# The first tiles of layer 0 in another order: statistics, transposed copies and PSUM banks

## The chip, the cores and the metric

The kernel runs on one core of a Trainium2 chip. Its engines work side by side, each on its own list of instructions in the order of the program: PE (TensorE, matrix products and transposes), DVE (VectorE), ACT (ScalarE), POOL (GpSimd), and SP, which here only issues DMAs. PE writes to PSUM, and a tile in PSUM can be overwritten only when DVE or ACT has read it. The metric is the device time of one execution in microseconds (us). It was 1230.78 us as the median of three runs, from 1225.78 to 1231.24.

## What is computed

Four layers, forward and backward, on x of 2048 rows by 512 columns: a linear attention block A, a gated block B, then A and B again with the same weights. Each adds to the residual stream. Outputs are the result and the gradients of x and of the five weight matrices.

```python
def _A_ref(x, wqkv, wo):                       # H = 32 heads, Dh = 16
    q, k, v = split(x @ wqkv)
    phi = lambda t: jnp.where(t > 0, t + 1, jnp.exp(t)) + 1e-6
    pq, pk = phi(q), phi(k)
    kv = jnp.einsum("bhsd,bhse->bhde", pk, v)
    z = jnp.einsum("bhsd->bhd", pk)
    o = einsum(pq, kv) / (einsum(pq, z)[..., None] + 1e-6)
    return o @ wo
def _B_ref(x, w_gate, w_up, w_down):
    return (_sigmoid(x @ w_gate) * (x @ w_up)) @ w_down
x = x + _A_ref(_layernorm(x), A_wqkv, A_wo)
x = x + _B_ref(_layernorm(x), B_w_gate, B_w_up, B_w_down)
...
_out, _vjp = jax.vjp(_f, A_x, A_wqkv, A_wo, B_w_gate, B_w_up, B_w_down)
return (_out, *_vjp(grad_out))
```

## The kernel before

The rows are cut into 16 tiles of 128. The change lies in `kq_fwd`, in the part that runs for layer 0 alone; this is the first thing that the kernel does. For each tile `st` it makes k and q from the normalised x, applies phi, and gathers X, the sum over all tiles of h-transposed times phi(k), from which the block's later matrices come.

One tile passes through these steps:

- `ln.stats(st)` (L436 to L442, in `ln_stats`): DVE takes the mean and variance in two instructions (L436, L438), then POOL makes of them, in three instructions, the reciprocal deviation (L439 and the power on L440) and the shift (L442).
- `ln.apply(st)` (L447): one ACT instruction writes the normalised tile into `h_all`.
- `stage_hT(sts, evac)`: PE transposes four blocks of 128 columns for each tile in `sts` into the PSUM tile `hT_tp` (L522), and one copy brings them to SBUF as `hTst`; it is made by DVE (L350, `evac` "vector") or by ACT (L352, "scalar"). `hT_tp` has one buffer, so that the next transposes wait for the copy. After the tile that ends a group of four a DMA stores the group (L585).
- `proj(st, 1)` and `proj(st, 0)`: four matmuls each (L591) for k and for q. They go into PSUM tiles handed out by `mm_tile` in the fixed turn t, t, y (two buffers of pool t, one of y).
- `exp_to` (L608): ACT takes the exponential of k, and another of q. `clamp` (L611): one DVE instruction for both halves of `a_t`, which has three buffers and is free again when its store to DRAM has landed. `phi_out` (L614): one DVE instruction for k and one for q; they also set the PSUM tiles free. `save_phq` (L617) stores the q half, and after tiles 2, 5, 8 and 11 the loads of later weights are issued behind that store.
- `X_some`: three or four X matmuls (L599) for tiles two back, into four PSUM tiles `X_ps` of the pools g and u.

No planner chooses the order: the engines' lists follow the order of calls in the loop. In iteration `st` the loop calls proj for k, the exponential of k, a staging of transposes (one tile at a time up to tile 3, then two at a time in odd iterations, copied by ACT), proj for q, the exponential of q, `ln.apply(st + 3)`, clamp and both phi, and then `ln.stats(st + 5)`. Before the loop stand the statistics of tiles 0 to 3 and the applies of 0 to 2; iteration 0 also runs `ln.stats(4)`. After the loop a sum of phi(k) over all rows (L708, 16 matmuls) goes into the next tile of the same turn of banks.

Of the kernel before, what the change touches and what calls it, by code (L numbers as in the profile page):

```python
# [10 lines left out]
F32 = mybir.dt.float32  # L11
# [7 lines left out]
D = 512  # L19
# [3 lines left out]
P = 128  # L23
NST = S // P
NDC = D // P
# [37 lines left out]
def ps_tile(k, which, shape, dt, name):  # L63
    return k.ps[which].tile(shape, dt, name=name, tag="ln_tp" if which == "ln" else f"{which}_ps")
# [3 lines left out]
def kernel(  # L68
# [78 lines left out]
    with tc.tile_pool(name="wfwd", bufs=1, reuse_waits="tile") as wfwd, ExitStack() as lctx, tc.manual_schedule(engines=EM):  # L147
# [44 lines left out]
        with tc.tile_pool(name="aq0", bufs=1, reuse_waits="tile") as aq:  # L192
            A = kq_fwd(k, aq, 0, lns[0], lns[1], x_bf)
            with tc.tile_pool(name="wt_stage", bufs=2, reuse_waits="tile") as wt_stage:
                fill = Fill(wT_groups_a(k, wt_stage))
                A.tail(fill)
                ab_fwd(k, A, lns[1], fill, nxt=lns[2])
        xctx.close()
        with tc.tile_pool(name="aq2", bufs=1, reuse_waits="tile") as aq:
            A = kq_fwd(k, aq, 2, lns[2], lns[3])  # L200
            hctx.close()
            wb = bctx.enter_context(tc.tile_pool(name="wbwd", bufs=1, side="right", reuse_waits="tile"))
# [340 lines left out]
def kq_fwd(k, aq, l, ln, ln_next, x_src=None):  # L543
# [10 lines left out]
    with ExitStack() as ctx:  # L554
# [13 lines left out]
        def mm_tile():  # L568
            nm = "tty"[cnt[0] % 3]
            cnt[0] += 1  # L570
            return ps_tile(k, nm, [P, D], F32, f"{nm}_mm")

        def stage_hT(sts, evac):
            st0 = sts[0]
            if st0 >= NST:
                return
            if st0 % NB == 0 or (st0 == 2 and ln.early):
                hTs["cur"] = stg.tile([P, NB, NDC, P], BF16, name="hTst")
            lo, n = st0 % NB, len(sts)
            for st in sts:  # L580
                hTs[st] = hTs["cur"][:, st % NB, :, :]
            ln.transposes(hTs["cur"][:, lo:lo + n, :, :].rearrange("p n c t -> p (n c) t"), sts, evac)
            if sts[-1] % NB == NB - 1:
                b, a = sts[-1] // NB, 2 if ln.early and sts[-1] < NB else 0
                nc.sync.dma_start(out=sv["hT"][(b * NB + a) * P:(b + 1) * NB * P, :].rearrange("(n p) d -> p n d", p=P),  # L585
                                  in_=hTs["cur"][:, a:NB, :, :].rearrange("p n c t -> p n (c t)"))

        def proj(st, n, ps=None):
            ps = ps or mm_tile()
            for kc in range(NDC):  # L590
                nc.tensor.matmul(ps[:], lhsT=hTs[st][:, kc, :], rhs=k.wqkv[:, kc, n * D:(n + 1) * D],  # L591
                                 start=(kc == 0), stop=(kc == NDC - 1))
            return ps

        X_ps = []
# [6 lines left out]
        def X_some(n, upto):  # L602
            while n > 0 and Xq and Xq[0][0] <= upto:
                X_mm(*Xq.pop(0))
                n -= 1

        def exp_to(e, ps):
            nc.scalar.activation(e, ps[:], ACT.Exp)  # L608

        def clamp(a, e):  # L610
            nc.vector.tensor_scalar(a, e, 1.0, EPS, ALU.min, ALU.add)  # L611

        def phi_out(out, ps, a):
            nc.vector.scalar_tensor_tensor(out, ps[:], 1.0 + EPS, a, ALU.add, ALU.max)  # L614

        def save_phq(st, a):
            ins = nc.sync.dma_start(out=sv["phq"][rows(st), :], in_=a)  # L617
            if l == 0 and st in k.late_loads:
                with tc.issue_after(ins.ins):
                    k.late_loads[st]()  # L620

        def store_pk(st):
            if st % NB == NB - 1:
                b = st // NB
                nc.sync.dma_start(out=dram_batch(sv["pk"], b), in_=pk_all[:, b * NB:(b + 1) * NB, :])

        def qa_tiles():
            if l == 0:
                return (work.tile([P, 2, D], BF16, name="e_t", bufs=2)[:, 1, :],
                        work.tile([P, 2, D], BF16, name="a_t", bufs=3)[:, 1, :])  # L630
            return (work.tile([P, D], BF16, name="e_t", bufs=4)[:],
                    work.tile([P, D], BF16, name="aq_t", bufs=4)[:])
# [12 lines left out]
        if l == 0:  # L645
            warm_ps = ps_tile(k, "g", [P, P], F32, "warm_ps")
            for i in range(WARM):
                nc.tensor.matmul(warm_ps[:], lhsT=k.ident[:], rhs=k.ident[:], start=True, stop=True)
            nc.scalar.activation(k.tab[:], k.neg[:], ACT.Exp)
            ln.stats(0)  # L650
            k.load_x()
            ln.stats(1)
            ln.apply(0)
            stage_hT([0], "vector")
            for st in range(2, 4):
                ln.stats(st)
            for st in range(1, 3):
                ln.apply(st)
        else:
            hTs.update(ln.early)  # L660
        X_ps += [ps_tile(k, "gu"[i % 2], [P, D], F32, "X_ps") for i in range(NDC)]
        for st in range(NST):
            both = st < NST - QLATE
            ps_k = proj(st, 1)
            if l == 0:
                e_t = work.tile([P, 2, D], BF16, name="e_t", bufs=2)
                a_t = work.tile([P, 2, D], BF16, name="a_t", bufs=3)
                ek, ak, eq, aqt = e_t[:, 0, :], a_t[:, 0, :], e_t[:, 1, :], a_t[:, 1, :]
            else:
                ek = work.tile([P, D], BF16, name="e_t", bufs=4)[:]  # L670
                ak = work.tile([P, D], BF16, name="ak_t", bufs=1)[:]
            exp_to(ek, ps_k)
            if l == 0 and st < 3:
                stage_hT([st + 1], "vector")
            elif l == 2 and st == 0:
                stage_hT([2, 3], "vector")
            elif st % 2 == 1 and st >= 3:
                stage_hT([st + 1, st + 2], "vector" if l == 2 and st % 4 == 1 else "scalar")
            if l == 2 or not both:
                clamp(ak, ek)  # L680
                phi_out(pk_all[:, st, :], ps_k, ak)
            if both:
                ps_q = proj(st, 0)
                if l == 2:
                    eq, aqt = qa_tiles()
                exp_to(eq, ps_q)
            if l == 0:
                ln.apply(st + 3)
                if both:
                    clamp(a_t[:], e_t[:])  # L690
                    phi_out(pk_all[:, st, :], ps_k, ak)
            elif st in (1, 2):
                ln.apply(NST - 3 + st)
            if both:
                if l == 2:
                    clamp(aqt, eq)
                phi_out(A.pq_all[:, st, :], ps_q, aqt)
                save_phq(st, aqt)
            if l == 0:
                if st == 0:  # L700
                    ln.stats(4)
                ln.stats(st + 5)
            store_pk(st)
            X_some(XSTEP + (st % 2 if l == 0 else 0), st - 2)

# [1002 lines left out]
```

## Time and profile before

| what | value |
|---|---|
| profiled execution's own time | 1234.76 us |
| its span | 1233.0 us |
| median of three runs | 1230.78 us |
| PE busy over the span | 1185.6 us, 96% |
| DVE, ACT, POOL busy | 731.7, 597.7, 258.4 us |
| first q,k matmul of layer 0 | at 7.19 us |
| sum of phi(k) begins (L708) | at 55.36 us |

The profile is one execution. The timeline lists instructions in order of start: start and duration in us, engine, line, operation, what is written and read. In brackets stands the idle time of the engine just before, and what ended it. PEld is the weight load of TensorE, SPq the issue of a DMA. The view by stretches gives for each engine its busy us and number of instructions, then the clock that TensorE was granted (1.00 is full), the share of the DMA engines and GB/s.

### The profile page before, as it was taken

To read this page: it belongs to the slowest core of one execution; us is meant where nothing else is said; L and a number is where in the kernel's file an instruction comes from. 1 tells how busy PE (TensorE), PEld (TensorE's weight loads), DVE (VectorE), ACT (ScalarE), POOL (GpSimd) and SP (SyncE) were. 2 spreads that over 40 slices of the span, in tenths; PEclk is the share of its full clock that TensorE was granted. 3 is DMA by queue.
4 is the path that set the end of the run, shared out by engine and by line. 5 is a ranking of instruction groups with operands and counts; after the bars stand their busy time and mean duration, and the time that the engine had idled before them with its cause. 6 is when DMAs were issued, how large, how long until landed. Compare 5 with 4: busy or idle time off the path is not lost.

```text
span 1233.0 us, 21735 instructions
## 1 busy us (share of the span) xinstructions
PE 1185.6 (96%) x8209; PEld 721.2 (58%) x8326; DVE 731.7 (59%) x1411; ACT 597.7 (48%) x1105; POOL 258.4 (21%) x469
## 2 busy tenths in 40 slices
PE   7989999998999999899999999999999999989998
PEld 4445555455555555455555578855557655537877
DVE  6688886777777456564966630156665947621111
ACT  5677777557676645344626631254445536610000
POOL 4246765105665300000100010000000101100000
PEclk9999999999999999999999999999999999998989
DMA  7934454435545867968665768568958765578773
GB/s 248 291 127 157 164 198 171 159 120 182 201 138 203 285 204 228 331 203 274 201 193 155 229 215 280 113 181 277 323 171 279 226 222 177 154 214 260 232 211 108
DMA packets 266233, 256.05 MB, mean 208 GB/s; under 512 B 43280, under 2 KB 251024, under 8 KB 261264
## 3 DMA queue, kind: packets, MB, share of 16 engines
q1 hardware_dynamic: 266128, 254.65, 64.6%
q8 instruction: 65, 1.06, 0.4%
q14 instruction: 40, 0.33, 0.1%
HBM read 135.69 MB, written 118.92 MB: 206 GB/s over the span
## 4 chain that ended last, share of the span: by engine, by line
PE 84%; DVE 8%; DMA 2%; issue 2%; SPq 2%; ACT 2%; POOL 1%; POOLq 0%; DVEq 0%; ACTq 0%
PE p_ps L1367 16%; PE dh_ps L1133 12%; PE g_ps L873 6%; PE u_ps L873 6%; PE y_ps L899 6%; PE dhh_ps L1017 6%; PE p_ps L1353 5%; PE dh_ps L1576 4%; PE T_ps L1092 3%; PE GT_ps L1494 2%; PE dp_ps L1469 2%; PE y_ps L818 2%; PE t_mm L591 2%; PE X_ps L599 2%; PE t_tp L887 1%
## 5 line engine op out<-in xcount | busy, mean ns | idle before, releaser
L1367 PE MATMUL p_ps<-p_set,p_a 128*128 128x256 bf16 (+1 forms) x2048 | 214.1, 266 | 3.5 <-DVE dw_stg L1343 3.5
L1367 PEld LDWEIGHTS <-p_a 128*128 128x128 bf16 x2048 | 186.9, 98 | 26.1 <-issue 3.6
L1025 DVE TENSOR_TENSOR dd<-dhh_ps,ssd 128x512 bf16<-128x512 f32 x144 | 82.5, 629 | 141.0 <-PE dhh_ps L1017 130.7
L1096 ACT COPY ddT<-T_ps 128x1024 bf16<-128x1024 bf16 (+1 forms) x96 | 83.0, 867 | 129.6 <-PE T_ps L1092 129.2
L879 POOL TENSOR_TENSOR ssd_t<-hh_t,oms 128x512 bf16<-128x512 bf16 (+1 forms) x96 | 101.6, 1064 | 53.3 <-ACT out_t L219 40.9
L1133 PEld LDWEIGHTS <-ddT 128*128 128x128 bf16 (+1 forms) x704 | 68.0, 98 | 70.0 <-issue 1.1
L991 POOL TENSOR_SCALAR ab<-c 128x2 f32<-128x2 f32 x64 | 12.3, 192 | 460.9 <-DVE junk L988 447.6
L873 PEld LDWEIGHTS <-hT 128*128 128x128 bf16 x768 | 71.2, 98 | 57.9 <-DVE hT L350 1.5
L1343 DVE TENSOR_TENSOR dw_stg<-p_ps,dw_stg 128x512 bf16<-128x512 f32 (+3 forms) x44 | 28.3, 648 | 125.1 <-PE p_ps L1367 85.6
L873 PE MATMUL g_ps<-wg,hT 128*128 128x512 bf16 (+1 forms) x378 | 88.9, 357 | 1.5 <-DVE hT L350 1.2
L873 PE MATMUL u_ps<-wu,hT 128*128 128x512 bf16 x383 | 89.8, 357 | 0.1
L878 DVE TENSOR_TENSOR hh_t<-u_ps,ssd_t 128x512 bf16<-128x512 f32 (+1 forms) x96 | 61.1, 636 | 46.9 <-PE u_ps L873 26.6
L1133 PE MATMUL dh_ps<-wgT,ddT 128*128 128x512 bf16 (+1 forms) x352 | 87.5, 383 | 0.0
L1353 PE MATMUL p_ps<-p_a,p_set 128*128 128x512 bf16 (+1 forms) x343 | 82.6, 388 | 1.4 <-DMA p_set<-sv_hdl 0.9
L983 ACT ACTIVATE t_sb<-dh_ps,rstd_all 128x512 f32<-128x512 f32 x64 | 44.0, 688 | 78.5 <-PE dh_ps L1576 52.4
L1133 PE MATMUL dh_ps<-wuT,ddT 128*128 128x512 bf16 (+1 forms) x351 | 81.2, 379 | 0.1
L899 PE MATMUL y_ps<-wd,hhT 128*128 128x512 bf16 (+1 forms) x327 | 76.2, 379 | 1.9 <-DVE x L901 0.6
L1017 PE MATMUL dhh_ps<-wdT,gT 128*128 128x512 bf16 (+1 forms) x341 | 75.8, 355 | 2.1 <-DVE dd L1025 0.5
L988 DVE SCALAR_TENSOR_TENSOR junk<-t_sb,h_ld 128x512 bf16<-128x512 f32 x64 | 44.0, 688 | 44.6 <-ACT t_sb L983 44.3
L875 ACT ACTIVATE ssd_t<-g_ps 128x512 bf16<-128x512 f32 (+1 forms) x96 | 53.2, 554 | 31.7 <-PE g_ps L873 31.5
L1345 ACT CAST dw_stg<-p_ps 128x512 bf16<-128x512 f32 (+2 forms) x43 | 24.1, 561 | 68.2 <-PE p_ps L1367 61.4
L1353 PEld LDWEIGHTS <-p_set 128*128 128x128 bf16 (+1 forms) x352 | 34.5, 103 | 38.0 <-issue 2.7
(230 smaller groups left out, 2132.8 us busy)
## 6 DMA issues: line engine op xcount, KB each, us to landing
p_set<-sv_hdd SPq DMA_DIRECT2D x30, 1024.0 KB, 6.3
sv_ssd<-ssd_t SPq DMA_DIRECT2D x32, 688.0 KB, 3.5
ssd<-sv_ssd SPq DMA_DIRECT2D x24, 688.0 KB, 5.1
sv_hdd<-dd SPq DMA_DIRECT2D x48, 320.0 KB, 4.1
sv_hdd<-hh_t SPq DMA_DIRECT2D x32, 320.0 KB, 2.6
h_ld<-sv_h SPq DMA_DIRECT2D x32, 256.0 KB, 4.6
p_a<-sv_h SPq DMA_DIRECT2D x16, 512.0 KB, 6.5
p_set<-sv_dqk SPq DMA_DIRECT2D x8, 1024.0 KB, 7.3
```

The costliest lines, as they stand in the source:

```text
L873: nc.tensor.matmul(ps[:, 0:w], lhsT=hT[:, kc, :], rhs=w_sb[:, kc, c0:c0 + w], start=(kc == 0), stop=(kc == NDC - 1))
L875: nc.scalar.activation(ssd_t[:, 0, c0:c0 + w], g_ps[:, 0:w], ACT.Sigmoid)
L878: nc.vector.tensor_tensor(hh_t[:, c0:c0 + w], u_ps[:, 0:w], ssd_t[:, 0, c0:c0 + w], ALU.mult)
L879: nc.gpsimd.tensor_tensor(ssd_t[:, 1, c0:c0 + w], hh_t[:, c0:c0 + w], oms[:, 0:w], ALU.mult)
L899: nc.tensor.matmul(y_ps[:], lhsT=T["hhT"][0:r, fc, :], rhs=k.wd[0:r, fc, :], start=(fc == 0), stop=(fc == NFC - 1))
L1017: k.nc.tensor.matmul(ps[:, 0:w], lhsT=gT[:, jc, :], rhs=k.wdT[:, jc, c0:c0 + w], start=(jc == 0), stop=(jc == NDC - 1))
L1025: k.nc.vector.tensor_tensor(dd[:, a, c0:c0 + w], ps[:, 0:w], ssd[:, a, c0:c0 + w], ALU.mult)
L1096: nc.scalar.copy(ddT[:, :, f0:f0 + nfull, :], tps[:, :, 0:nfull, :])
L1133: nc.tensor.matmul(T["dh"][:], lhsT=ddT_block(T, a, fc), rhs=(k.wuT, k.wgT)[a][0:r, fc, :], start=(i == 0), stop=(i == 2 * NFC - 1))
L1353: nc.tensor.matmul(ps[0:r, :], lhsT=set_t[:, st, c * P:c * P + r], rhs=self.ops[j["l"], "g"][:, st, :], start=(st == 0), stop=(st == NST - 1))
L1367: nc.tensor.matmul(ps[:, icl * w:(icl + 1) * w], lhsT=self.ops[j["l"], "h"][:, st, ic * P:(ic + 1) * P], rhs=set_t[:, st, 0:w], start=(st ...
L1576: nc.tensor.matmul(dh_ps[:], lhsT=lhsT, rhs=rhs, start=(i == 0), stop=(i == len(ops) - 1))
```

## The change

Five edits, all in `kq_fwd`, all for layer 0 but the place where `X_ps` is taken:

1. The statistics of tile 2 are called ahead of the transposes of tile 0; those of tile 3 stay behind them.
2. The transposes of tile 2 are called in iteration 0 behind the exponential of q, those of tile 3 in iteration 1. Their copies to SBUF, which DVE made, are made by ACT.
3. q of tile 1 goes to a buffer of the PSUM pool u, outside of the turn t, t, y.
4. `X_ps` is taken in iteration 2 and not ahead of the loop.
5. Iteration `st` calls `ln.stats(st + 4)`; it called `ln.stats(st + 5)`, and iteration 0 also `ln.stats(4)`. `ln.apply(st + 3)` stays where it is.

```diff
             ln.stats(1)
             ln.apply(0)
+            ln.stats(2)
             stage_hT([0], "vector")
-            for st in range(2, 4):
-                ln.stats(st)
+            ln.stats(3)
             for st in range(1, 3):
                 ln.apply(st)
         else:
             hTs.update(ln.early)
-        X_ps += [ps_tile(k, "gu"[i % 2], [P, D], F32, "X_ps") for i in range(NDC)]
         for st in range(NST):
+            if st == 2:
+                X_ps += [ps_tile(k, "gu"[i % 2], [P, D], F32, "X_ps") for i in range(NDC)]
             both = st < NST - QLATE
             ps_k = proj(st, 1)
...
             exp_to(ek, ps_k)
-            if l == 0 and st < 3:
-                stage_hT([st + 1], "vector")
+            if l == 0 and st < 2:
+                stage_hT([2 * st + 1], "scalar" if st else "vector")
             elif l == 2 and st == 0:
                 stage_hT([2, 3], "vector")
...
             if both:
-                ps_q = proj(st, 0)
+                ps_q = proj(st, 0, ps_tile(k, "u", [P, D], F32, "u_mm") if st == 1 else None)
                 if l == 2:
                     eq, aqt = qa_tiles()
                 exp_to(eq, ps_q)
             if l == 0:
+                if st == 0:
+                    stage_hT([2], "scalar")
                 ln.apply(st + 3)
...
             if l == 0:
-                if st == 0:
-                    ln.stats(4)
-                ln.stats(st + 5)
+                ln.stats(st + 4)
             store_pk(st)
```

## The prediction

> **What bounds the kernel now.** I read the page's head first, then the waits of the first 60 us, then the timeline there.
>
> ```profile
> span 1233.0 us, 21735 instructions
> PE 1185.6 (96%) x8209; PEld 721.2 (58%) x8326; DVE 731.7 (59%) x1411; ACT 597.7 (48%) x1105; POOL 258.4 (21%) x469
> ```
>
> PE is the bound as a whole, so a change in layer 0's k/q loop counts by how much earlier or later PE gets through it. That loop ends where the sum of phi(k) starts, at 55.36. Ahead of tile 2 PE starves; from there the loop runs at full pace:
>
> ```profile
> 5.41 0.81 ACT L447 ACTIVATE h_all<-x_bf,ln_nmr,rstd_all 128x512 bf16<-128x512 bf16 x1 [3.11 <-POOL x_bf L161]
> 6.27 0.40 PE L522 MATMUL hT_tp<-ident,h_all 128*128 128x128 bf16 x4 [0.42 <-ACT h_all L447]
> 6.71 0.43 DVE L350 COPY hTst<-hT_tp 128x512 bf16<-128x512 bf16 x1 [0.96 <-PE hT_tp L522]
> ...
> 9.01 0.27 POOL L442 TENSOR_SCALAR ln_nmr<-ln_mv,rstd_all 128x1 f32<-128x1 f32 x1
> 9.31 0.81 ACT L447 ACTIVATE h_all<-x_bf,ln_nmr,rstd_all 128x512 bf16<-128x512 bf16 x1 [1.38 <-POOL ln_nmr L442]
> ...
> 12.34 1.02 PE L591 MATMUL t_mm<-wqkv,hTst 128*128 128x512 bf16 x4 [1.76 <-DVE pk_all L614]
> ...
> 15.03 1.89 PE L591 MATMUL t_mm<-wqkv,hTst 128*128 128x512 bf16 x4 [1.67 <-DVE hTst L350]
> ```
>
> The edits aim at the last two waits: q of tile 1 waits for a bank, k of tile 2 for a copy queued on DVE. Now two tiles of the steady loop, from the clamp of tile 5 to that of tile 7:
>
> ```profile
> 28.11 0.43 DVE L611 TENSOR_SCALAR a_t<-e_t 128x1024 bf16<-128x1024 bf16 x1 [0.28 <-ACT e_t L608]
> ...
> 29.78 0.68 DVE L436 BATCH_NORM_STATS2 ln_stats<-x_bf 128x6 f32<-128x512 bf16 x1
> ...
> 30.87 0.80 ACT L447 ACTIVATE h_all<-x_bf,ln_nmr,rstd_all 128x512 bf16<-128x512 bf16 x1
> ...
> 31.13 0.72 POOL L440 TENSOR_TENSOR rstd_all<-rstd_all,neghalf 128x1 f32<-128x1 f32 x1
> ...
> 31.96 0.27 POOL L442 TENSOR_SCALAR ln_nmr<-ln_mv,rstd_all 128x1 f32<-128x1 f32 x1
> ...
> 32.38 1.01 ACT L352 COPY hTst<-hT_tp 128x1024 bf16<-128x1024 bf16 x1
> ...
> 33.27 0.61 ACT L608 ACTIVATE e_t<-t_mm 128x512 bf16<-128x512 f32 x1
> ...
> 33.77 0.82 ACT L447 ACTIVATE h_all<-x_bf,ln_nmr,rstd_all 128x512 bf16<-128x512 bf16 x1
> 33.92 0.43 DVE L611 TENSOR_SCALAR a_t<-e_t 128x1024 bf16<-128x1024 bf16 x1 [0.28 <-ACT e_t L608]
> ```
>
> Two tiles take 33.92 - 28.11 = 5.81 us. The statistics at 29.78 are those of tile 10; their shift is ready at 32.23, and the apply that uses it starts at 33.77, 1.54 later. That slack is why the loop never waits for statistics:
>
> ```profile
> ACT h_all L447 <- POOL ln_nmr L442: 3.8, 3, 1.5
> ```
>
> Three times, all ahead of 16 us. One more row matters, from the chain that ended last: the clamp of tile 12 waits until 49.19 for a store to land that was issued at 40.19, in a stretch where the DMA engines are over 90% busy. It should have come at 45.55 + 2.91 = 48.46, so the wait costs 0.73.
>
> **The change, part by part.**
>
> *Start (edits 1 to 4): a gain.* I follow the new order with these rows. Statistics of tile 2 (two DVE instructions, 0.69 and 0.18) fit into DVE's idle 0.96 ahead of 6.71; its POOL work can start behind tile 1's at 7.12, takes 0.31 + 0.68 + 0.30, and its apply starts at 8.41 where it started at 9.31. Two exponentials follow on ACT (apply to exponential 0.70, exponential to the next instruction 0.49): 9.11 and 9.60. Then tile 2's copy, now on ACT. The nearest row is 0.59 for an ACT copy of 128x512 out of PSUM at 62.73, against DVE's 0.39 to 0.43; it holds ACT for 0.48, 10.09 to 10.57. Apply of tile 3 at 10.57, exponential of k1 at 11.27. Transposes of tile 3 at 10.57 + 0.87 = 11.44, copied at 11.88 on ACT; q1 needs no bank and starts at 11.70, its exponential 1.07 later (row: 30.82 to 31.89), clamp of tile 1 at 12.77 + 0.65 = 13.42. It stood at 14.88: gain 1.46. Its ends: both ACT copies at the full 0.59 and shift to apply at 0.54 (14.93 to 15.47) give 13.9, and so does tile 4's statistics, queued on DVE ahead of this clamp, if its load (issued at 5.4) is not there before 12.95, where that step ran before: gain 1.0. An ACT copy at DVE's 0.39 gives 1.55. The moved store of the first four transposed tiles (one DMA) passes tile 1's store on SP's queue; SP idles there from 12.41 to 15.33, so it costs nothing. X's fourth bank now waits for phi of q1 at about 15.3; its first use is in iteration 3, later. The turn of banks stands one place on behind tile 1; each projection still waits for the one three places back, and the sum of phi(k) lands in y, free at 59.60 and next needed at 63.27. Both cost nothing.
>
> *Edit 5: a loss that repeats.* No instruction is added, but each statistics call comes one tile (2.91) later, and the slack was 1.54. The apply would be 1.37 late, and on ACT's list the next exponential of k and the copy stand behind it; on PE the second tile's transposes wait for it, and with them q. So a cycle closes over two tiles, from an odd tile's clamp to the next odd tile's:
>
> - clamp to shift instruction: 31.96 - 28.11 = 3.85
> - shift to apply: 9.31 - 9.01 = 0.30
> - apply to transposes: 6.27 - 5.41 = 0.86
> - four transposes to copy: 6.71 - 6.27 = 0.44
> - copy to exponential of q: 33.27 - 32.38 = 0.89
> - exponential to clamp: 33.92 - 33.27 = 0.65
>
> Sum 6.99 in place of 5.81. (The even cycle, 3.85 + 0.30 + 0.70 + 0.49 + 0.65 = 5.99, is shorter.) Low end 6.75: the power at 0.57 as at 8.34 and the statistics at 0.73 a step as at 12.95. High end 7.25: shift to apply 0.54 as above. I take 6.99, the rows of the loop itself. There are six such cycles, clamp 1 to clamp 13: 13.42 + 6.83 (the first has an idle DVE beside the power, 0.57) + 5 x 6.99 = 55.20. Before it is 52.09, the 0.73 of the store included. That store has 10.5 us in the longer loop and took 8.91, so I leave its wait out: loss 3.1.
>
> *Behind the loop.* From clamp 13 on both have the same PE list, 55.36 - 52.09 = 3.27. Weight loads hang on the stores of tiles 5, 8 and 11; the last moves from 46.38 to about 49.1, takes 8.1, and is used behind 74. Nothing there waits for a clock of its own, so the loss goes through to the end.
>
> Sum: 1234.76 + 3.1 = 1237.9 for an execution like the profiled one. The runs' median lies 3.98 lower, so 1230.78 + 3.1 gives 1233.9.
>
> **Clock.** In stretches of 3.41 us the trace shows
>
> ```profile
> 11.43:14.84 3.41, 1.02 (x4) 0.29 (x3) 3.23 (x8) 1.45 (x3) 0.79 (x2) 1.00 0.72 235
> 14.84:18.25 3.41, 3.23 (x11) 1.47 (x12) 2.90 (x7) 1.41 (x2) 2.20 (x6) 0.50 0.13 43
> 48.97:52.39 3.42, 2.70 (x19) 1.45 (x19) 2.02 (x4) 2.24 (x4) 0.00 (x0) 1.00 0.88 261
> ```
>
> PE busy 1.02 of 3.41 was followed by half clock, 2.70 was not. The new loop idles about 6.99 - 5.81 = 1.2 at a time, which leaves 2.2 of 3.41, so I expect full clock. The first such wait is longer (transposes of tile 5, about 16.0 to 18.2); if it falls whole into one stretch, half clock costs 1.71 less the waiting of about 0.6 in a stretch: up to 1.1 more.
>
> **Rivals.**
>
> *A, forecast:* as above, 1233.9. Low end: start 0.1 and cycles 1.4 less, 1232.4. High end: start 0.5, cycles 1.6, clock 1.1 and the store's 0.7 more, 1237.8.
>
> *B, faster:* the loop keeps 5.81. Then the start's gain of about 1.5 stays: 1229.3. It decides when the odd cycle falls by 1.18, for instance if the shift were ready 2.97 behind the clamp and not 4.15. For it: the start has real waits. Against: every link is a row, and none is that much too long.
>
> *C, the clock swings:* short waits at every pair of tiles bring half clock again and again. Each cold stretch takes 1.71 of PE; the waiting in two stretches gives back 1.2 x 6.83 / 6.99 = 1.17; six times 0.54 makes 3.2 more, 1237.1, with the first wait up to 1238.2. Against: 2.70 busy kept the clock. The Trainium skill, TensorE: Matmul & The Clock Gate, section A second HAM failure mode: psum-queue depth-cycling, says that short idles between groups of matmuls can make the clock swing between half and full. By it the time would be C's; this trace shows no swing at such waits.
>
> *D, nothing:* the waits at the start were hidden and the slack suffices: 1230.8. Against: the 1.67 and 1.76 above are PE's own.
>
> **Numbers.** A 0.72, B 0.08, C 0.13, D 0.07. Half a per cent, 6.2 us, is about what runs that spread over 5.5 can tell from no change. A and D lie within it, but A, with its high end or the runs' spread, passes 1236.9 in about one case of seven (0.10), and C mostly (0.11). B passes 1224.6 only at the low end of the spread. Slower 0.21, same 0.75, faster 0.04. Range 1228.5 to 1239.5: from B to C with the runs' spread.
>
> **What would show it.** Right: clamp 1 near 13.4; statistics, POOL, apply, transposes, copy and exponential of q in a closed chain; ACT waiting for POOL's shift about a dozen times; 7.0 between odd clamps; sum of phi(k) near 58.5. Wrong: clamps 5.8 apart, TensorE at half clock inside the loop, or the sum of phi(k) ahead of 55.4.

## The result and the profile after

The changed kernel takes 1234.09 us as the median of 20 runs, from 1230.39 to 1238.94; the kernel before, beside it, 1230.35 (20 runs, 1225.78 to 1236.27). The ratio is 1.0034, 95% interval 1.0019 to 1.0049: slower by 4.2 us, between 2.3 and 6.0.

The page of the changed kernel begins:

```profile
span 1231.1 us, 21736 instructions
PE 1183.1 (96%) x8209; PEld 720.0 (58%) x8326; DVE 730.9 (59%) x1409; ACT 599.0 (49%) x1107; POOL 257.4 (21%) x469
```

Its span is 1.9 us shorter than the 1233.0 of the profiled execution before, though the kernel is slower. The two executions are not alike elsewhere: counted in stretches of 1 us, TensorE ran 23.9 us at half clock in the one before and 17.1 in this one (at 14, 509, 1107 and 1195 before; at 20, 282 and 1108 after). So I don't compare spans but the place where the change acts: the start of the sum of phi(k), the first work behind the loop, which I call the mark. It lies 4.20 later than the 55.36 of before, and the first product of the last matrix of block B starts at 93.66 in place of 89.44, 4.22 later, so that the delay is handed on. In the timeline:

```profile
59.56 3.62 PE L709 MATMUL y_mm<-pk_all,ones_sq 128*128 128x512 bf16 x16
```

The waits of the first 64 us show what is new (total, times, longest):

```profile
ACT h_all L447 <- POOL ln_nmr L442: 10.7, 11, 2.0
PEld L522 <- ACT h_all L447: 9.0, 7, 2.2
PE hT_tp L522 <- ACT h_all L447: 7.2, 7, 2.0
```

ACT waited for the shift 3 times before and waits 11 times now; PE's transposes waited once for an apply and wait 7 times now. One turn of the loop, in the timeline from the clamp of tile 9 to that of tile 11:

```profile
42.34 0.43 DVE L611 TENSOR_SCALAR a_t<-e_t 128x1024 bf16<-128x1024 bf16 x1 [1.47 <-ACT e_t L608]
...
44.01 0.68 DVE L436 BATCH_NORM_STATS2 ln_stats<-x_bf 128x6 f32<-128x512 bf16 x1
...
45.37 0.72 POOL L440 TENSOR_TENSOR rstd_all<-rstd_all,neghalf 128x1 f32<-128x1 f32 x1
...
46.20 0.26 POOL L442 TENSOR_SCALAR ln_nmr<-ln_mv,rstd_all 128x1 f32<-128x1 f32 x1
...
46.50 0.81 ACT L447 ACTIVATE h_all<-x_bf,ln_nmr,rstd_all 128x512 bf16<-128x512 bf16 x1 [1.29 <-POOL ln_nmr L442]
...
47.37 0.40 PE L522 MATMUL hT_tp<-ident,h_all 128*128 128x128 bf16 x4 [1.06 <-ACT h_all L447]
...
47.80 1.01 ACT L352 COPY hTst<-hT_tp 128x1024 bf16<-128x1024 bf16 x1
...
48.71 0.60 ACT L608 ACTIVATE e_t<-t_mm 128x512 bf16<-128x512 f32 x1
...
49.34 0.43 DVE L611 TENSOR_SCALAR a_t<-e_t 128x1024 bf16<-128x1024 bf16 x1 [1.47 <-ACT e_t L608]
```

This is the chain of the prediction. From the clamp to the shift instruction (L442) it takes 3.86, then from row to row 0.30, 0.87, 0.43, 0.91 and 0.63, together 7.00. The prediction had 3.85, 0.30, 0.86, 0.44, 0.89, 0.65. Odd clamps stand at 14.44, 21.53, 28.38, 35.23, 42.34, 49.34 and 56.34: six turns in 41.90.

The start went otherwise than predicted. Two loads are waited for there, in the timeline and, last row, in the chain that ended last:

```profile
9.16 1.02 PE L591 MATMUL t_mm<-wqkv,hTst 128*128 128x512 bf16 x4 [0.47 <-DMA wqkv<-in_A_wqkv_dram]
...
13.61 0.69 DVE L436 BATCH_NORM_STATS2 ln_stats<-x_bf 128x6 f32<-128x512 bf16 x1 [1.01 <-DMA x_bf<-in_A_x_dram]
...
14.44 0.39 DVE L611 TENSOR_SCALAR a_t<-e_t 128x1024 bf16<-128x1024 bf16 x1
```

```profile
5.36 8.16 DMA x_bf<-in_A_x_dram
```

Clamp 1 comes at 14.44, only 0.44 ahead of before.

### The profile page after: what moved, and what is told of

The parts are those of the page before. It is cut to its first block, busy times and chain, and to the rows that moved or that the text cites. A ratio compares the mean times of both kernels' runs of the same rounds, so it can differ in the third digit from the quotient of the medians.

```text
span 1231.1 us, 21736 instructions
## 1 busy us (share of the span) xinstructions
PE 1183.1 (96%) x8209; PEld 720.0 (58%) x8326; DVE 730.9 (59%) x1409; ACT 599.0 (49%) x1107; POOL 257.4 (21%) x469
## 4 chain that ended last, share of the span: by engine, by line
PE 85%; DVE 8%; DMA 3%; issue 2%; ACT 1%; POOL 1%; SPq 1%; DVEq 0%; POOLq 0%; ACTq 0%
PE p_ps L1368 16%; PE dh_ps L1134 12%; PE p_ps L1354 6%; PE u_ps L874 6%; PE g_ps L874 6%; PE y_ps L900 6%; PE dhh_ps L1018 6%; PE dh_ps L1577 4%; PE T_ps L1093 3%; PE GT_ps L1495 2%; PE dp_ps L1470 2%; PE y_ps L819 2%; PE t_mm L591 2%; PE t_tp L888 1%; PE X_ps L599 1%
## 5 line engine op out<-in xcount | busy, mean ns | idle before, releaser
L1368 PE MATMUL p_ps<-p_set,p_a 128*128 128x256 bf16 (+1 forms) x2048 | 211.2, 264 | 2.3 <-DVE dw_stg L1344 2.3
```

The lines of the kernel that those rows point to most:

```text
L1368: nc.tensor.matmul(ps[:, icl * w:(icl + 1) * w], lhsT=self.ops[j["l"], "h"][:, st, ic * P:(ic + 1) * P], rhs=set_t[:, st, 0:w], start=(st ...
```

## Experiments

Each was timed beside the kernel before. Clamps and "phi sum", the mark, are from one profiled execution of each. For the kernels with the old lead (before, e1, e7, e8, e10) and for e3 and e5 "odd clamps apart" gives the steady turns; the first, and in most of them the last, is of another length.

| kernel | clamp 1 | odd clamps apart | phi sum | ratio to before, 95% interval |
|---|---|---|---|---|
| before | 14.88 | 5.81 | 55.36 | 1 |
| changed | 14.44 | 6.85 to 7.11 | 59.56 | 1.0034 (1.0019 to 1.0049) |
| e1, edit 5 undone | 14.94 | 5.81 | 53.64 | 0.9977 (0.9965 to 0.9990) |
| e2, edit 5 alone | 14.46 | 6.79 to 7.04 | 59.51 | 1.0042 (1.0026 to 1.0058) |
| e5, even tiles late | 14.88 | 6.34 | 55.33 | 0.9994 (0.9980 to 1.0008) |
| e6, odd tiles late | 13.76 | 6.78 to 7.00 | 58.23 | 1.0007 (0.9990 to 1.0025) |
| e9, odd tiles late, on before | 14.01 | 6.87 to 7.01 | 58.74 | 1.0031 (1.0016 to 1.0045) |
| e3, transposes by single tiles | 13.56 | 6.46 to 6.47 | 56.07 | 1.0007 (0.9991 to 1.0023) |
| e4, rows of tile 4 first | 13.54 | 7.00 to 7.06 | 58.90 | 1.0029 (1.0018 to 1.0041) |
| e10, rows of tile 4 first, on before | 15.25 | 5.82 | 56.69 | 0.9981 (0.9966 to 0.9996) |
| e7, e1 and e4 together | 13.67 | 5.81 | 52.04 | 0.9970 (0.9958 to 0.9982) |
| e8, e7 with later weight loads | 13.74 | 5.81 | 51.59 | 0.9954 (0.9938 to 0.9969) |

### The two halves of the change (e1, e2)

e1 is the changed kernel with its last edit undone:

```diff
             if l == 0:
-                ln.stats(st + 4)
+                if st == 0:
+                    ln.stats(4)
+                ln.stats(st + 5)
```

> The changed kernel with its fifth edit alone undone: the loop calls the statistics of tile st + 5 again, iteration 0 also those of tile 4; the four edits of the start stay. Theory A (the later statistics close a cycle of about 7.0 us over two tiles, from an odd tile's clamp to the next odd tile's): odd clamps 5.8 apart again, the sum of phi(k) starts at 53.2 to 54 where it stood at 55.36 before and at 59.56 after the change, and the time is 1.3 to 2.2 us under the kernel before, ratio 0.998 to 0.999. Rival S (the start is to blame: copies on ACT, the bank of pool u, the late load of rows 512 to 1023): the sum of phi(k) stays at 58 to 60 and the time about 4 us over the kernel before.

e2 is the kernel before with that edit alone, the other way round.

> The kernel before with the fifth edit alone: statistics of tile st + 4 in iteration st, nothing else changed. Theory A: odd clamps 7.0 apart, six times, clamp 1 near 14.8 as before, the sum of phi(k) at 59.5 to 60.5, time 4 to 5 us over the kernel before, ratio about 1.0035. Rival S: clamps 5.8 apart, the sum of phi(k) at 55 to 56, ratio 1.000.

Measured: phi sum at 53.64 and a ratio of 0.9977 without the edit, 59.51 and 1.0042 with the edit alone. The loss is edit 5's: 4.15 at the mark on the old start (55.36 to 59.51) and 5.92 on the new one (53.64 to 59.56). The rival that blamed the start falls.

What the four edits of the start are worth is less clear. With the old lead they gain 1.72 at the mark, and the timed gain of 2.8 us, between 1.2 and 4.3, contains it; beside edit 5 they gain nothing at the mark (59.51 in e2, 59.56 in the changed kernel). Nor does the gain of e1 come where the prediction put it. Clamps 1 and 3 of the kernel before, with the statistics that stand ahead of clamp 1 on DVE,

```profile
13.78 0.66 DVE L436 BATCH_NORM_STATS2 ln_stats<-x_bf 128x6 f32<-128x512 bf16 x1
...
14.88 0.42 DVE L611 TENSOR_SCALAR a_t<-e_t 128x1024 bf16<-128x1024 bf16 x1
...
22.30 0.43 DVE L611 TENSOR_SCALAR a_t<-e_t 128x1024 bf16<-128x1024 bf16 x1 [0.28 <-ACT e_t L608]
```

and of e1:

```profile
14.15 0.66 DVE L436 BATCH_NORM_STATS2 ln_stats<-x_bf 128x6 f32<-128x512 bf16 x1
...
14.94 0.39 DVE L611 TENSOR_SCALAR a_t<-e_t 128x1024 bf16<-128x1024 bf16 x1
...
20.49 0.43 DVE L611 TENSOR_SCALAR a_t<-e_t 128x1024 bf16<-128x1024 bf16 x1 [0.26 <-ACT e_t L608]
```

Clamp 1 is not earlier in e1. In both kernels it stands on DVE behind the statistics of tile 5, which edit 5 moves behind it. The gain comes in the next turn, 5.55 against 7.42, and there the kernel before ran at half clock from 14.84 to 18.25. Of the four profiled executions with the old start, two fell to half clock there (before and e10) and two did not (e2 and e9); of the three with the new start and the old lead (e1, e7, e8) none did. How much of the 1.72 is clock, and whether the new start prevents it, is not shown.

In e1 the kernel meets the other wait that the prediction names, that for a store, in the waits of 64 us and in the chain:

```profile
DVE a_t L611 <- DMA sv_phq<-a_t: 2.0, 1, 2.0
```

```profile
38.38 9.00 DMA sv_phq<-a_t
```

It was 8.91 long before. Clamp 12 comes 0.83 late for it in e1 and came 0.73 late before.

### Which tile's lateness counts (e5, e6, e9)

e5 calls the statistics in pairs in even iterations, so that only even tiles are late; e6 in odd iterations, so that only odd tiles are; e9 is e6's edit on the kernel before.

```diff
-            if l == 0:
-                ln.stats(st + 4)
+            if l == 0 and st % 2 == 0:        # e5
+                ln.stats(st + 4)
+                ln.stats(st + 5)
```

```diff
             if l == 0:
-                ln.stats(st + 4)
+                if st == 0:                   # e6, and e9 on the kernel before
+                    ln.stats(4)
+                elif st % 2 == 1:
+                    ln.stats(st + 4)
+                    ln.stats(st + 5)
```

> The changed kernel with the statistics called in pairs in even iterations: those of the even tile st + 4 as late as in the changed kernel, those of the odd tile st + 5 as early as in the kernel before. Theory A, which needs the odd tile (its transposes stand ahead of q on PE and its copy ahead of the exponential of q on ACT): only the shorter even cycle is left, 6.0 to 6.4 over two tiles, the sum of phi(k) at 55.5 to 56.5, ratio to before about 1.0005. Rival T (a late apply holds up ACT whatever tile it is for): about half of the loss or more stays, 7.0 over two tiles, the sum of phi(k) at 58 to 60.

> The changed kernel with the statistics called in pairs in odd iterations from iteration 1 on: those of the odd tile st + 4 as late as in the changed kernel, those of the even tile st + 5 as early as in the kernel before. Theory A: the odd cycle of 7.0 over two tiles stays whole though half of the statistics are early, the sum of phi(k) at 59 to 60, ratio to before about 1.0035. Rival T: half of the loss is gone, the sum of phi(k) at 56 to 57.5.

> The kernel before with nothing changed but the statistics: called in pairs in odd iterations, odd tiles as late as in the changed kernel, even tiles as early as before. Theory A (the odd tile alone closes the cycle): odd clamps 6.9 to 7.0 apart, the sum of phi(k) at 58.5 to 60.2, ratio to before 1.0025 to 1.004, as in the kernel with all statistics late. Rival T (each late statistic adds its part): half of the loss, the sum of phi(k) near 57.4 and the ratio 1.0015 to 1.002. The odd-late run on the changed start gave 58.23 and a ratio of 1.0007, between the two.

Clamps in the timeline, of e5:

```profile
33.56 0.45 DVE L611 TENSOR_SCALAR a_t<-e_t 128x1024 bf16<-128x1024 bf16 x1
36.48 0.43 DVE L611 TENSOR_SCALAR a_t<-e_t 128x1024 bf16<-128x1024 bf16 x1 [1.14 <-ACT e_t L608]
39.90 0.45 DVE L611 TENSOR_SCALAR a_t<-e_t 128x1024 bf16<-128x1024 bf16 x1
```

The third stands directly behind the statistics of two tiles, of which the second is

```profile
39.03 0.66 DVE L436 BATCH_NORM_STATS2 ln_stats<-x_bf 128x6 f32<-128x512 bf16 x1
39.80 0.18 DVE L438 BATCH_NORM_AGGREGATE ln_mv<-ln_stats 128x2 f32<-128x6 f32 x1
```

Of e6:

```profile
34.30 0.43 DVE L611 TENSOR_SCALAR a_t<-e_t 128x1024 bf16<-128x1024 bf16 x1 [1.68 <-ACT e_t L608]
38.08 0.45 DVE L611 TENSOR_SCALAR a_t<-e_t 128x1024 bf16<-128x1024 bf16 x1
41.14 0.43 DVE L611 TENSOR_SCALAR a_t<-e_t 128x1024 bf16<-128x1024 bf16 x1 [1.28 <-ACT e_t L608]
```

Two tiles take 39.90 - 33.56 = 6.34 with even tiles late and 41.14 - 34.30 = 6.84 with odd tiles late. About the same number of statistics are late in both. The 6.34 lies in the expected range, but not for the expected reason: the odd clamp of e5 has no idle time ahead of it, so it waits for DVE itself, which in e5 has two statistics in a row to do. Its exponential started at 38.75, so that by the 0.65 of the prediction it could have come at 39.40, 0.50 earlier, and the turn would be 5.84, an estimate. In e6 the odd clamps wait for ACT with DVE idle, so there the pair of statistics is not what sets them. What differs is PE's wait for an apply, in the waits of e5 first and then of e6:

```profile
PE hT_tp L522 <- ACT h_all L447: 2.3, 3, 1.0
```

```profile
PE hT_tp L522 <- ACT h_all L447: 7.6, 7, 2.0
```

The odd tile is the second of its pair, and the pair's copy waits for it. The length of the turns speaks for the closed cycle, and so does e9, whose phi sum of 58.74 and ratio of 1.0031 are what was expected, though the interval of the ratio begins at 1.0016 and does not rule out the rival's 1.0015 to 1.002; the mark, against 57.4, does. Two marks lie outside of what was expected: e5's 55.33 just below 55.5, and e6's 58.23 below 59, since its clamp 1 came 0.68 earlier than in the changed kernel and its turns were a little shorter. The ratio of e6 was a miss too: 1.0007, where its mark (2.87 later than before) would make 1.0023, just inside its interval. By times alone e6 would have spoken for the rival that half of the loss goes; that is why e9 was run.

### Where the cycle closes (e3)

From iteration 3 on the transposes are staged for one tile at a time; statistics stay late for all.

```diff
-            elif st % 2 == 1 and st >= 3:
+            elif l == 0 and st >= 3:
+                stage_hT([st + 1], "scalar")
+            elif l == 2 and st % 2 == 1 and st >= 3:
                 stage_hT([st + 1, st + 2], ...)
```

> The changed kernel with the transposes of layer 0 staged for one tile in every iteration from iteration 3 on, where two tiles were staged in odd iterations; statistics as late as in the changed kernel. Theory A: transposes no longer wait for the tile whose apply has just run, so the cycle closes only over ACT (apply, exponential of k, copy, exponential of q): 3.85 + 0.30 + 0.70 + 0.49 + 0.48 + 0.65 = 6.5 over two tiles, the sum of phi(k) near 57, ratio to before 1.001 to 1.002. If the loop is held by something else than this chain, for instance by the DMA engines, it stays at 7.0 and the sum of phi(k) at 59 to 60.

In the timeline of e3, from the clamp of tile 8 to that of tile 10, with the apply that uses the statistics called behind clamp 8:

```profile
36.29 0.43 DVE L611 TENSOR_SCALAR a_t<-e_t 128x1024 bf16<-128x1024 bf16 x1 [0.93 <-ACT e_t L608]
...
40.45 0.81 ACT L447 ACTIVATE h_all<-x_bf,ln_nmr,rstd_all 128x512 bf16<-128x512 bf16 x1 [1.29 <-POOL ln_nmr L442]
...
41.17 0.58 ACT L608 ACTIVATE e_t<-t_mm 128x512 bf16<-128x512 f32 x1
...
41.64 0.57 ACT L352 COPY hTst<-hT_tp 128x512 bf16<-128x512 bf16 x1
...
42.11 0.61 ACT L608 ACTIVATE e_t<-y_mm 128x512 bf16<-128x512 f32 x1
...
42.75 0.43 DVE L611 TENSOR_SCALAR a_t<-e_t 128x1024 bf16<-128x1024 bf16 x1 [0.93 <-ACT e_t L608]
```

Two tiles take 6.46, against an expected 6.5, and from the apply to the exponential of q every link is on ACT. The turn is 0.5 shorter than with pairs, but little of that is the way over PE. From the apply to the copy it is 1.19 here (0.72 + 0.47) and was 1.30 over the transposes; from the copy to the exponential of q it is 0.47 and was 0.91, because the copy of one tile is half as large. So the pair costs 0.11 by its transposes and 0.44 by its copy, and the other links agree within 0.01.

Phi sum is at 56.07 where 57 was expected: clamp 1 came at 13.56, 0.88 ahead of the changed kernel's, though the start is the same code. Behind clamp 13 e3 takes 3.96 where the changed kernel took 3.22. The ratio of 1.0007 is below the expected 1.001 to 1.002, which its interval contains.

### The loads of the start (e4, e10)

One element written by POOL holds back a load of x. In the changed kernel it lies in rows 512 to 1023, so that tile 4's load, named ahead of the two later ones, is issued behind them at 5.36. e4 moves the hold to those two; e10 does it on the kernel before.

```diff
-            nc.gpsimd.memset(x_bf[0:1, NB, 0:1], 0.0)
+            nc.gpsimd.memset(x_bf[0:1, 2 * NB::NB, 0:1], 0.0)
```

> The changed kernel, but the one-element write of POOL that holds a load of x back until tile 0's statistics are done is moved from the rows 512 to 1023 to the two later groups of rows, so that tile 4's load is issued at about 2.8 and not at 5.4. Theory A says that the gain of the start was mis-sized because tile 4's statistics waited for this load on DVE until 13.61 and held clamp 1 to 14.44: without it clamp 1 comes at 13.9 to 14.1, and the sum of phi(k) 0.3 to 0.5 earlier than the changed kernel's 59.56; too little for the time to tell. If instead the late weights of q (waited for until 9.16) or ACT set clamp 1, it stays at 14.4.

> The kernel before with the hold of x moved alone. Its statistics of tile 4 ran at 12.95 without a wait of their own, so the load was hardly late there: clamp 1 stays at 14.5 to 14.9, the sum of phi(k) within 0.5 of 55.36 or, without a stretch at half clock in the first 60 us, near 54.4; ratio 0.9985 to 1.000. If the load held the kernel before as well, the ratio comes near 0.997, that of the moved hold together with the new start, and the new start's own edits are worth nothing.

In e4 tile 4's statistics run without a wait behind phi of tile 0, and the clamp follows the exponential:

```profile
12.07 0.68 DVE L436 BATCH_NORM_STATS2 ln_stats<-x_bf 128x6 f32<-128x512 bf16 x1
...
13.54 0.43 DVE L611 TENSOR_SCALAR a_t<-e_t 128x1024 bf16<-128x1024 bf16 x1 [0.57 <-ACT e_t L608]
```

Clamp 1 comes at 13.54. The wait for q's weights, 0.5 in the changed kernel, is not listed in e4 either, which is why it comes earlier than the 13.9 to 14.1 expected. Phi sum is 0.66 earlier than in the changed kernel, a little more than expected; the turns of the loop stay 7.0 long.

One execution doesn't say what the moved hold is worth, since loads land at another time in each. e3 has the start of the changed kernel, with the hold where it was, and its clamp 1 comes just as early though it still waits for the rows:

```profile
12.73 0.69 DVE L436 BATCH_NORM_STATS2 ln_stats<-x_bf 128x6 f32<-128x512 bf16 x1 [0.91 <-DMA x_bf<-in_A_x_dram]
...
13.56 0.40 DVE L611 TENSOR_SCALAR a_t<-e_t 128x1024 bf16<-128x1024 bf16 x1
```

The wait itself is in every execution of the new start with the hold in the old place (0.61 to 1.07 in the changed kernel, e1, e3, e5 and e6) and in none with the moved one (e4, e7, e8). With the old lead, clamp 1 comes at 13.67 (e7) and 13.74 (e8) with the rows first, against 14.94 in e1.

e10 stays open. Its ratio, 0.9981, is a gain of 2.3 us (0.5 to 4.2), a little more than expected, and its interval holds both the expected 0.9985 and the rival's 0.997. Its profiled execution shows no gain and misses what was expected: half clock for 6.8 us from 13.8 on, clamp 1 at 15.25 and a phi sum of 56.69. What the moved hold is worth to the kernel before can't be read from one execution with that stretch in it.

### Both kernels beaten (e7, e8)

e7 joins e1 and e4. e8 adds that the two large weight loads are issued behind the stores of tiles 12 and 13:

```diff
-            8: lambda: nc.sync.dma_start(out=k.wu[:], ...),
-            11: load_wd,
+            12: lambda: nc.sync.dma_start(out=k.wu[:], ...),
+            13: load_wd,
```

> The moved hold of the load of x together with the undone fifth edit: the start of the changed kernel, the statistics' lead of the kernel before, and tile 4's load first. Theory A: clamp 1 near 14.2, odd clamps 5.8 apart, the sum of phi(k) at 52.1 to 53.2, time 2.2 to 3.3 us under the kernel before, ratio 0.997 to 0.998; the store that held tile 12's clamp for 0.73 in the kernel before may hold it again and longer, since stores come earlier and the weights' loads with them.

> The kernel with the moved hold and the lead put back, and in addition the two large weight loads of the gated block issued behind the stores of tiles 12 and 13 and not 8 and 11. If the clamp of tile 12 waits (it came 3.40 behind clamp 11 in that kernel, against 2.90 between others) because its buffer's store stands behind the 1.4 MB load, clamp 12 now comes 2.9 behind clamp 11, and the sum of phi(k) at about 51.5 in place of 52.04; the time falls by 0.5 us, ratio to before about 0.9966, if the weights still land ahead of their first use behind 70. If they do not, the first gate and up products wait and the time is higher than that of the kernel without this edit (0.997).

Clamps 11 and 12 in the timeline, of e7:

```profile
42.47 0.43 DVE L611 TENSOR_SCALAR a_t<-e_t 128x1024 bf16<-128x1024 bf16 x1 [0.28 <-ACT e_t L608]
45.87 0.43 DVE L611 TENSOR_SCALAR a_t<-e_t 128x1024 bf16<-128x1024 bf16 x1 [1.65 <-DMA sv_phq<-a_t]
```

and of e8:

```profile
42.53 0.43 DVE L611 TENSOR_SCALAR a_t<-e_t 128x1024 bf16<-128x1024 bf16 x1 [0.28 <-ACT e_t L608]
45.43 0.43 DVE L611 TENSOR_SCALAR a_t<-e_t 128x1024 bf16<-128x1024 bf16 x1 [1.15 <-ACT e_t L608]
```

3.40 becomes 2.90: the store had stood behind the weight load. Phi sum: 52.04 in e7, 51.59 in e8, both about as expected. e7's ratio is 0.9970, as expected, and e8's 0.9954, better than the expected 0.9966, with a median of 1226.14 us against 1230.97. The intervals of the two overlap, so that the step from e7 to e8 is shown at the mark and not in the times. e8 beats the kernel before by 0.46% (0.31 to 0.62) and so the changed one too.

## Why the prediction was right, and where not

**The loop: right, in mechanism and size.** The cycle was predicted at 6.99 and the six turns at 41.78; they take 41.90. Every link of it is within 0.02 of its row. e1 and e2 put the loss on edit 5, and e6 and e9 show that late statistics of odd tiles alone keep nearly the whole turn (6.84 to 6.88 in the steady loop, against 7.00). e3 shows that the staging of a pair lengthens the turn, by its copy above all. One number of the prediction stays without a test: the even cycle of 5.99, since e5 was held by DVE.

**The start: the gain was mis-sized.** The prediction had clamp 1 at 13.42 with ends 13.3 and 13.9; it came at 14.44, so the gain was 0.44 and not 1.46. Three things went otherwise.

- It let q of tile 0 run as before, with the exponential at 9.60. q's weights were waited for until 9.16 and the exponential came at 10.22. That made the exponential of q1 13.36 in place of 12.77, clamp 14.01. This differs from execution to execution: PE was free for q at 8.69, later than the 8.46 at which it ran without a wait before. With the same order e3, e4 and e6 do not wait for these weights, and e1, e5 and e7 wait 0.2 to 0.4.
- Then tile 4's statistics, queued on DVE ahead of the clamp, waited for their rows until 13.61 and pushed it to 14.44. The prediction named this load and bounded it by 12.95, the time when that step ran before; but that row had no wait in it and said nothing of when the load lands in another execution. Here it landed 8.16 behind its issue, 7.33 in e6 and 7.79 in e1.
- It booked the whole gain on edits 1 to 4, but set it against a clamp 1 at 14.88 that stood on DVE behind the statistics of tile 5 (from 13.78 on). Edit 5 moves these behind the clamp. With edit 5 alone (e2) clamp 1 comes at 14.46, with edits 1 to 4 alone (e1) at 14.94: so the 0.44 of the changed kernel is not shown to be a gain of the start.

**The sum, and luck in it.** Loss at the mark 4.20 where 3.1 was predicted. The missing 1.02 of the start is nearly the whole difference; the turns add 0.12 and the stretch behind them takes 3.22 in place of 3.27. The timed loss is 4.2, but that mark and time agree so well is partly luck: the mark of before belongs to one execution whose first turn took 7.42 where the steady turns took 5.81, with half clock in it, and a loss of 4.20 counts from there. The six turns take 41.90 where six steady ones of before make 34.86, which is 7.04 more; of this 1.61 was in the first turn of before already, 0.73 in its wait for the store, and 0.44 came off at clamp 1. The predicted median of 1233.9 is closer to 1234.09 than the sum deserves, because the runs' median of the kernel before moved from 1230.78 to 1230.35 with more runs, and because 3.74 between the medians is less than the 4.2 of the ratio.

**What was to cost nothing.** The bank of pool u, the late X banks, the turn of banks and the moved store show no wait in the changed kernel. The clamp of tile 12 no longer waits for its store, as taken. The last weight load is issued at 50.17 (about 49.1 was predicted) and nothing waits for it.

**The clock.** Rival C, the clock that swings, did not happen in the loop: one stretch at half clock, from 20.0 on, behind the first long wait (PE idle from 17.24 to 19.25), as the prediction allowed for. In stretches of 1 us:

```profile
18.00:19.00 1.00, 0.00 (x0) 0.00 (x0) 0.96 (x3) 0.62 (x1) 0.30 (x1) 1.00 0.00 1
...
21.00:22.00 1.00, 1.00 (x4) 0.37 (x3) 0.44 (x2) 0.78 (x2) 0.57 (x2) 0.50 1.03 361
...
24.00:25.00 1.00, 1.00 (x6) 0.46 (x5) 0.17 (x1) 0.73 (x2) 0.66 (x2) 1.00 0.97 346
```

It lies in the turns of 7.09 and 6.85 that end at 21.53 and 28.38. The first was predicted at 6.83, but e4 takes 7.06 for it without half clock, so the clock lengthened the loop little, if at all.

The rule behind rival C can be read closer from the 12 traces, cut into the clock's own stretches of 3.41 us. In them, up to 1220 us, a stretch at full clock with PE busy 1.39 or less was always followed by half clock, one with 1.9 or more never, and between the two both happened. The slow loop keeps PE busy 2.3 in its emptier stretches (2.27 in the changed kernel, 2.31 to 2.36 in e2), so by these counts its waits are too short for half clock; the stretch ahead of 20.0 had 1.15. The Trainium skill, TensorE: Matmul & The Clock Gate, section A second HAM failure mode: psum-queue depth-cycling, tells of a kernel whose short idles between groups of matmuls make the clock swing. This trace shows no such swing at waits of 1.1 us in every 7.

## What to carry to other kernels

When work runs a fixed number of tiles ahead, read its slack from the steady loop (here 1.54 us between the shift and its use) and compare it with one tile (2.91) before the lead is shortened. If it falls short, add up the closed chain: it sets the new pace for the whole loop, and a gain at the start is paid once while the chain is paid at every turn. In a start that waits for loads, a row that shows no wait gives no landing time: take the issue and the time to landing, and allow for its spread (here 7.3 to 8.2 us for one load). And when a gain is booked on one part of a change, ask whether another part moves the row that it is measured from.

## What was not expected

Single executions of one kernel differ by more than this change: 1230.39 to 1238.94 in 20 runs of the changed kernel, and the time largely follows the mean clock that TensorE was granted: both runs of 1238.94 had 0.990, those with 0.996 or 0.997 lay between 1230.39 and 1233.52. In the profiles half clock comes in stretches of 3.4 us and multiples (3.4, 6.8, 10.2), and their sum goes from 6.8 us in e6 to 23.9 in the kernel before, e3 and e10. A stretch at half clock was followed by another one whenever PE was busy 2.68 or less of its 3.41, and by full clock from 2.90 on. So the shorter of two profiled spans belonged to the slower kernel, and a mark in the trace behind the changed part told more than the span.
